# A fused MLP forward and backward: one load for each tile of x in two queues, w1's first part divided, and Gelu's table moved

## The chip, the cores and the metric

The kernel runs on one core of a Trainium2 chip. The metric is the device time of one execution in microseconds (us), the median of several runs; lower is better. The core has a matrix engine (TensorE, PE in the profile; PEld is its loading of weights), a vector engine (VectorE, DVE), an engine for activation functions (ScalarE, ACT), a general one (GpSimd, POOL) and a queue engine that only issues transfers (SyncE, SP). Transfers (DMA) are issued here by SP and by ScalarE, each in a queue of its own, in order.

## The reference

A two-layer MLP with the tanh form of Gelu, and the gradients of all its inputs, in bfloat16, with 2048 rows, width 448 and hidden width 1792:

```python
def _fwd_reference(x, w1, b1, w2, b2):
    h = jnp.einsum("bsd,df->bsf", x, w1) + b1
    h = _gelu(h)
    return jnp.einsum("bsf,fd->bsd", h, w2) + b2

def reference(x, w1, b1, w2, b2, grad_out):
    _out, _vjp = jax.vjp(_f, x, w1, b1, w2, b2)
    return (_out, *_vjp(grad_out))      # out, gx, gw1, gb1, gw2, gb2
```

## The kernel before

The hidden width is cut into 14 tiles of 128, taken two at a time (a pair, 7 of them), and the rows into 4 blocks of 512. That gives 28 pairs p = 0 to 27. For each pair there is a step `u` (x times w1 into PSUM), a bias copy `c` into a buffer, Gelu `g` on ScalarE, a step `p` or `o` (h times w2), a step `q` (the gradient times w2 transposed), the derivative of Gelu on ScalarE and VectorE (`s e r y t z m n G`), and `x` (the gradient of h times w1 transposed). The weight gradients follow at the end, with full 128-row matmuls (L798, L852).

The order on each engine is written out by hand in five strings: `PE_ORDER`, `ACT_ORDER`, `DVE_ORDER`, `SP_ORDER` and a few names for GpSimd. An engine runs its string from left to right and waits where an input is not there or a buffer is not free. Nothing is reordered. A step `u2.1` is pair 2, first of two runs (d = 1), `u2.2` its second (d = 2). The width of 448 is not a multiple of 128, so TensorE works with its array cut into two halves of 64 rows; two matmuls of a run stand side by side, and a run has 4 such pairs of matmuls for d = 1 and 3 for d = 2 while p is below 7.

This case is about the start. Pair 0 is not done as `u0` with 512 columns but as `h0` and `h1`, with 256 columns each (the first and the second 256 rows of x), so that it can begin before all of the first block is there. The names at the start:

- `xr01`: the load of tile 0 of x (128 rows, 112 KB) into `x_rows`; `xr12` is tile 1, `xr24` tiles 2 and 3 in one load. They are issued by the engine in whose string they stand.
- `X0` to `X3` in `PE_ORDER`: TensorE turns a tile of x with an identity matrix into two PSUM banks: `X_BANKS = ((0, 1), (2, 3), (6, 7), (0, 1))`. `X3` uses the banks of `X0`.
- `X0.0`, `X0.1` and so on in the strings of VectorE and ScalarE: the copy of one of the two banks into `xT` (L600). VectorE has X0.0 X1.0 X3.0 X3.1, ScalarE X0.1 X1.1 X2.0 X2.1.
- `W6`: six matmuls with ones, to have TensorE running; `F6` and `f4`: fills, six and four pairs of small matmuls with ones into PSUM columns that nothing reads.
- `L0` to `L4`: w1's five parts by columns (256, 256, 256, 256, 768), for pairs 0, 1, 2, 3 and 4 to 6. `Z0` to `Z2`: the rest of w1's rows, by `REST_COLS`; a step `u` of the first block needs the `L` and the `Z` of its pair.
- `K`, `J`, `I`: parts of w2, w2 transposed and w1 transposed. `b1` is loaded by SP, turned by TensorE in `B`, and copied by VectorE as `b1T`; the bias copies `c0A0` (ScalarE) and `c0B0` (VectorE) need it.
- `table`: an ACTIVATE of one column with Gelu, so that the table of the function is loaded early.
- `HOLD`: a load named in it waits until another one has landed. Here `L1` (`w11m`), issued by SP, waits for the first rows of x (`xrows0`), and SP issues nothing else meanwhile.

`Nx` and `Ng` (`rows_nat`, L732) load all of x and of grad_out again, for the weight gradients, in two halves each.

Of the kernel before, what the change touches and what calls it, by code (L numbers as in the profile page):

```python
# [88 lines left out]


PE_ORDER = """
W6 X0 X1 F6 X2 X3 h0.1 f4 h0.2 B h1.1 u1.1 h1.2 u1.2 u2.1 u3.1 u2.2 u3.2 p0.0 p0.1 p0.2 p0.3 p1.0 p1.1 u4.1 u5.1 u4.2 u5.2
p1.2 p1.3 p2.0 p2.1 p2.2 p2.3 u6.1 p3.0 u6.2 p3.1 p3.2 p3.3 p4.0 p4.1 u7.1 p4.2 u7.2 p4.3 p5.0 p5.1 p5.2 p5.3 u8.1
p6.0 u8.2 q0.1 p6.1 q0.2 u9.1 p6.2 u9.2 q1.1 p6.3 q1.2 u10.1 o1.0.0.6.1 u10.2 q2.1 o1.1.0.6.1 u11.1 q2.2 u11.2
o1.0.0.6.2 o1.1.0.6.2 q3.1 u12.1 q3.2 u12.2 o1.0.6.10.1 q4.1 o1.1.6.10.1 u13.1 q4.2 u13.2 o1.0.6.10.2 q5.1 o1.1.6.10.2
# [11 lines left out]
x3.1.6.10.1 x3.0.6.10.2 x3.1.6.10.2 x3.0.10.14.1 x3.1.10.14.1 x3.0.10.14.2 x3.1.10.14.2  # L107
"""
ACT_ORDER = """
xr12 L0 Z0 table X0.1 X1.1 X2.0 X2.1 c0A0 c0A1 s0 g0 s1 g1 c2B t0 s2 g2 g3 s3 c5B g4 t1 t2 c6B g5 g6 s4 s5 g7 c8A c8B g8 c9A c9B  # L110
g9 c10A c10B t3 t4 g10 s6 c11A c11B s7 g11 t5 c12A c12B g12 s8 t6 c13A c13B g13 s9 t7 s10 t8 c14A c14B t9 g14 s11 s12
c15A c15B t10 g15 c16A c16B s13 t11 g16 c17A c17B s14 t12 g17 c18A c18B s15 g18 vx0.2 c19A c19B t13 t14 g19 s16 c20A
c20B s17 g20 t15 s18 t16 s19 c21A c21B t17 g21 c22A c22B s20 t18 g22 c23A c23B g23 s21 t19 s22 t20 s23 c24A c24B t21
# [12 lines left out]
vx3.3  # L126
"""
SP_ORDER = """
xr01 xr24 b1 L1 Z1 L2 L3 K0 K1 L4 Z2 K2 K3 X1 R F b2 Y0 J0 J1 J2 Y1 I0 E J3 I1 So0.1 So0.0 X2 H0 H1 H2 H3 H4 H5 H6 H7 H8 H9
T0 T1 H10 T2 H11 T3 H12 T4 H13 T5 So1.0 So1.1 T6 T7 H14 T8 Y2 H15 T9 X3 H16 T10 H17 Sx0.0 Sx0.1 T11 H18 H19 T12 H20  # L130
T13 T14 T15 So2.0 Y3 H21 So2.1 T16 H22 H23 T17 T18 T19 H24 Sx1.0 T20 Sx1.1 H25 T21 H26 Nx H27 T22 T23 Sx2.0 Sx2.1 T24
T25 T26 So3.0 So3.1 Ng T27 Sx3.0 Sx3.1
# [28 lines left out]
def make_plan(tc, ctx, x, w1, b1, w2, b2, grad_out, out_0, out_1, out_2, out_3, out_4, out_5):  # L161
    nc = tc.nc
    P = 128
    _, S, D = x.shape
    F = w1.shape[1]
# [3 lines left out]
    MAIN = 3 * P  # L169
# [201 lines left out]
    def fill(n, bks, c0):  # L371
        def fn():
            run(n * [[(bks[i], (c0, P), one[64 * i:64 * i + 64, 0:P], one[64 * i:64 * i + 64, 0:P], True, True) for i in (0, 1)]], True)
        pe("fill", fn, [], [bank(("fill", len(pl.lists["PE"]), i), bks[i]) for i in (0, 1)], ("s128", n), (bks, 1))
# [143 lines left out]
        return {"SP": nc.sync, "ACT": nc.scalar, "POOL": nc.gpsimd}[eng]  # L518

    loads = {}  # L520
    HOLD = {"w11m": "xrows0"}

    def dma(eng, name, out, in_, reads, writes, nbytes):
        def fn():
            d = loads[name] = dq(eng).dma_start(out=out, in_=in_)
# [82 lines left out]
        v += [val((tag[0] + "e", b), (tag + "e", b % 2))] if b > 0 else []  # L608
        turn_rows(f"{tag}{b}.{hs[0]}", dst[b % 2][:, :, EDGE + c0 - e:EDGE + c0 + n], src, b * SB + c0 - e, n + e, v, tag if b == NB - 1 else None)

    def LW1(part, eng="SP"):
        c0, c1 = W1_COLS[part]
        v = [("w1", part)]
        dma(eng, f"w1{part}m", w1_sb[:, 0:3, c0:c1], w1[0:MAIN, c0:c1].rearrange("(k p) f -> p k f", p=P), [], v, (c1 - c0) * 768)

    def LW1Z(part, eng="SP"):

# [40 lines left out]
    def num(t):  # L658
        return [int(i) for i in t.split(".")]

    for t in PE_ORDER.split():
        k, a = t[0], t[1:]
        if k == "w":
            wake(int(a), P)
        elif k == "W":
            wake(int(a))
        elif k == "X":
            XT(int(a))
        elif k == "f":
            fill(int(a), (3, 2), 2 * P)  # L670
        elif k == "F":
            fill(int(a), (6, 7), 2 * P)
        elif k == "B":
            pe("b1u", lambda: nc.tensor.matmul(bk_(6)[:, 0:16], lhsT=b1n[0:64, :], rhs=ident[0:64, 0:16], start=True, stop=True,  # L674
                                               skip_group_check=True), ["b1n", "b1z", "ident"], [bank(("b1u",), 6)], ("s16", 1), (None, 0))
# [22 lines left out]
    for eng, order in (("ACT", ACT_ORDER), ("DVE", DVE_ORDER)):  # L698
        for t in order.split():
            k, a = t[0], t[1:]  # L700
            if k == "c":
                hf = None if a[-1] in "AB" else int(a[-1])
                a = a if hf is None else a[:-1]
                C(int(a[:-1]), "AB".index(a[-1]), eng, hf)
            elif k == "v":
                EV(a[0], *num(a[1:]), eng)
            elif k == "L":
                LW1(int(a), eng)
            elif k == "Z":
                LW1Z(int(a), eng)  # L710
            elif t[:2] == "xr":
                LXN(int(t[2]), int(t[3]), eng)
            elif t == "ident":
                pl.op(eng, "ident", identity, ["identz"], ["ident"], ("tiny", 1))
            elif k == "X":
                XC(*num(a), eng)
            elif k == "D":
                LED({"x": "xT", "g": "gT"}[a[0]])
            elif k == "K":
                LW2(int(a), eng)  # L720
            elif t in ("b1", "b2"):
                (LB1 if t == "b1" else LB2)(eng)
            elif t == "b1T":
                pl.op(eng, "b1T", b1_turn, [("b1u",)], ["b1T"], ("tiny", 4))
            elif t == "table":
                pl.op(eng, "table", lambda: nc.scalar.activation(out=tiny[:], in_=one[:, 0:1], func=ACT.Gelu_apprx_tanh), [], ["tiny"], ("table", 1))
# [66 lines left out]
    for ft in range(NF):  # L793
# [7 lines left out]
        eng = "ACT"  # L801
# [94 lines left out]
```

## Time and profile before

| | |
|---|---|
| median of 3 runs | 264.36 us (264.32 to 264.71) |
| profiled execution | 264.21 us |
| its span, first to last instruction | 262.4 us |
| TensorE busy | 259.0 us (99%) |
| VectorE busy | 199.3 us (76%) |
| ScalarE busy | 127.3 us (48%) |
| DMA | 46.61 MB, mean 178 GB/s |

The span is what the profiler saw between the first and the last instruction; the execution's own time has about 1.8 us around it. A row of a timeline gives the start in us from the span's start, the duration, the engine (a q behind it: its queue, issuing), the line of the kernel, the operation, what it writes and reads, its shape (64*128 64x512: a weight of 64 by 128 against 512 columns), how many instructions were merged, and in brackets the idle time before it and what ended it. A row of stretches gives, for each, its length and each engine's busy time. In `qb` lie PSUM banks 6 and 7; `bank` is any of the other six; `TR` holds x's first rows at the start; `w1f` holds w1, `gh_nat` at first the rest of its rows (`Z`).

### The profile page before, as it was taken

The numbers are of one execution on the slowest core, as the hardware profiler recorded it, in microseconds if no ns is written. First come the engines' busy times: TensorE is split into PE (matmuls) and PEld (weight loads), VectorE is DVE, ScalarE is ACT, GpSimd is POOL, SyncE is SP. The second block draws the span as 40 slices with busy tenths as digits, with TensorE's granted clock in tenths as the row PEclk, the third lists the DMA queues.
The fourth block names the chain that finished last, engine by engine and source line by source line (L and its number), as shares of the span: only waits on it lengthen the run. The fifth ranks groups of instructions, "written<-read, shape, count | busy, mean of one in ns | idle before, by whom it ended". The sixth has DMA issues, their size and how long they took to land.

```text
span 262.4 us, 5411 instructions
## 1 busy us (share of the span) xinstructions
PE 259.0 (99%) x2217; PEld 149.0 (57%) x2217; DVE 199.3 (76%) x286; ACT 127.3 (48%) x165; POOL 14.2 (5%) x11
## 2 busy tenths in 40 slices
PE   8999999999999999999999999999999999999995
PEld 4444455555555666666666677765555555555554
DVE  5898398999999989999997995249999999310000
ACT  4899569846898956875896310011121111000001
POOL 1000000000000000000000000000000392400000
PEclk9999999999999999999999999999999999999999
DMA  6999999999999892992387825984799989877221
GB/s 187 306 261 147 204 134 152 244 352 215 256 208 220 233 232 45 163 235 43 102 207 250 222 42 62 243 238 95 157 238 125 180 194 179 200 179 178 72 70 35
DMA packets 120633, 46.61 MB, mean 178 GB/s; under 512 B 96686, under 2 KB 120479, under 8 KB 120608
## 3 DMA queue, kind: packets, MB, share of 16 engines
q1 hardware_dynamic: 119920, 45.82, 79.1%
q10 hardware_dynamic: 688, 0.44, 0.5%
q8 instruction: 17, 0.28, 0.4%
q14 instruction: 8, 0.07, 0.1%
HBM read 8.20 MB, written 14.28 MB: 86 GB/s over the span
## 4 chain that ended last, share of the span: by engine, by line
PE 99%; ACT 0%; issue 0%
PE bank L242 48%; PE qb L242 18%; PE bank L798 16%; PE bank L852 16%; PE qb L368 1%; ACT w_sb L857 0%; PE qb L674 0%
## 5 line engine op out<-in xcount | busy, mean ns | idle before, releaser
L242 PEld LDWEIGHTS <-HG 64*128 64x128 bf16 x896 | 55.6, 94 | 32.2 <-POOLq L236 1.9
L242 PE MATMUL qb<-gT,w2Tf 64*128 64x512 bf16 x392 | 52.9, 376 | 0.0
L242 PE MATMUL bank<-w_sb,HG 64*128 64x448 bf16 x448 | 48.4, 349 | 0.0
L242 PE MATMUL bank<-xT,w1f 64*128 64x512 bf16 (+1 forms) x360 | 47.6, 370 | 0.0
L242 PE MATMUL bank<-w1T_sb,HG 64*128 64x448 bf16 x448 | 47.2, 349 | 0.0
L482 DVE SCALAR_TENSOR_TENSOR HG<-TR,qb 128x1024 bf16<-128x1024 bf16 x28 | 34.1, 1218 | 12.6 <-PE qb L242 12.5
L852 PE MATMUL bank<-w2Tf,HG 128*128 128x448 bf16 (+2 forms) x240 | 42.6, 340 | 0.0
L798 PE MATMUL bank<-w1f,gh_nat 128*128 128x448 bf16 x224 | 42.5, 352 | 0.0
L852 PEld LDWEIGHTS <-HG 128*128 128x128 bf16 x240 | 22.9, 98 | 19.8
L798 PEld LDWEIGHTS <-gh_nat 128*128 128x128 bf16 x224 | 21.8, 98 | 20.6 <-issue 0.4
L242 PEld LDWEIGHTS <-w2Tf 64*128 64x128 bf16 x392 | 24.1, 94 | 16.6 <-POOLq L236 0.3
L467 ACT ACTIVATE TR<-TR 128x1024 bf16<-128x1024 bf16 x28 | 29.1, 1052 | 6.6 <-DVE TR L457 6.6
L242 PEld LDWEIGHTS <-w1f 64*128 64x128 bf16 x382 | 21.7, 94 | 17.7 <-DMA w1f<-in_w_dram 0.7
L821 DVE TENSOR_TENSOR w1T_sb<-w1T_sb,gh_nat 128x1792 f32<-128x1792 f32 x14 | 28.4, 2026 | 0.5
L803 ACT ACTIVATE TR<-bank 128x448 bf16<-128x448 f32 x14 | 7.6, 543 | 34.9 <-PE bank L798 34.9
L858 DVE CAST w_sb<-bank 128x448 bf16<-128x448 f32 x6 | 3.7, 623 | 25.9 <-PE bank L852 25.9
L857 ACT CAST w_sb<-bank 128x448 bf16<-128x448 f32 (+2 forms) x9 | 4.4, 490 | 37.7 <-PE bank L852 37.7
L827 POOL PARTITION_ALL_REDUCE w1T_sb<-w1T_sb x1 | 10.6, 10568 | 206.2 <-DVE w1T_sb L825 206.2
L442 ACT ACTIVATE TR<-gh_nat 128x1024 bf16<-128x1024 bf16 x15 | 15.7, 1052 | 11.5 <-DVE TR L477 11.5
L472 DVE TENSOR_SCALAR TR<-TR 128x2048 bf16<-128x2048 bf16 x28 | 19.2, 688 | 1.9 <-ACT TR L467 1.9
L462 DVE TENSOR_TENSOR TR<-TR,HG 128x1024 bf16<-128x1024 bf16 x28 | 19.2, 684 | 0.0
L477 DVE TENSOR_TENSOR TR<-TR 128x1024 bf16<-128x1024 bf16 x28 | 19.0, 686 | 0.1
(55 smaller groups left out, 188.9 us busy)
## 6 DMA issues: line engine op xcount, KB each, us to landing
hT_dram<-HG SPq DMA_DIRECT2D x28, 256.0 KB, 3.0
out_dram<-st SPq DMA_DIRECT2D x16, 224.0 KB, 2.8
w1f<-in_x_dram SPq DMA_DIRECT2D x2, 896.0 KB, 5.9
w2Tf<-in_grad_out_dram SPq DMA_DIRECT2D x2, 896.0 KB, 6.4
out_dram<-w_sb SPq DMA_DIRECT2D x2, 448.0 KB, 3.0
out_dram<-xT SPq DMA_DIRECT2D x2, 384.0 KB, 3.2
w_sb<-in_w_dram SPq DMA_DIRECT2D x1, 672.0 KB
w1f<-in_w_dram SPq DMA_DIRECT2D x3, 192.0 KB, 3.7
```

The source lines that it names most:

```text
L242: m = nc.tensor.matmul(bk_(b)[:, at:at + n], lhsT=l, rhs=r, start=st, stop=sp, skip_group_check=True)
L442: pl.op("ACT", f"s{p}", lambda: nc.scalar.activation(out=TR[p % NTR][:, 1], in_=ubuf(p), func=ACT.Square, scale=sc), [("ub", p)], [v], ("a ...
L462: pl.op("DVE", f"R{p}", lambda: nc.vector.tensor_tensor(out=t[:, 1], in0=t[:, 1], in1=hblk(p), op=ALU.mult), [("r", p), ("h", p)], [val((" ...
L467: pl.op("ACT", f"t{p}", lambda: nc.scalar.activation(out=t[:, 0], in_=t[:, 0], func=ACT.Tanh), [("y", p)], [val(("t", p), ("TR0", p % NTR) ...
L472: pl.op("DVE", f"m{p}", lambda: nc.vector.tensor_scalar(out=t[:], in0=t[:], scalar1=1.0, scalar2=None, op0=ALU.subtract), [("t", p), ("r2" ...
L477: pl.op("DVE", f"n{p}", lambda: nc.vector.tensor_tensor(out=t[:, 0], in0=t[:, 0], in1=t[:, 1], op=ALU.mult), [("m0", p), ("m1", p)], [val( ...
L482: pl.op("DVE", f"G{p}", lambda: nc.vector.scalar_tensor_tensor(out=ghblk(p), in0=t[:, 0], scalar=2.0, in1=qb[:, :, :], op0=ALU.subtract, o ...
L798: nc.tensor.matmul(bk_(bk)[:, 0:D], lhsT=gh_nat[:, st // 4, ft, st % 4, :], rhs=x_nat[:, st, :], start=(st == 0), stop=(st == NS - 1))
L803: fn = (lambda dst=dst, src=src: nc.scalar.mul(out=dst, in_=src, mul=-0.5)) if eng == "ACT" else \
L821: nc.vector.tensor_tensor(out=hs3, in0=a, in1=gh_nat[:, st // 4, :, st % 4, :], op=ALU.add)
L827: pl.op("POOL", "gb1", lambda: nc.gpsimd.partition_all_reduce(gb1_w, hsum, channels=P, reduce_op=bass_isa.ReduceOp.add), ["hsc"], ["gb1"], ...
L852: nc.tensor.matmul(bk_(bk)[:, 0:d1 - d0], lhsT=h_nat[ft][:, st, :], rhs=g_nat[:, st, d0:d1], start=(st == 0), stop=(st == NS - 1))
```

## The change

- x's four tiles are loaded by one load each: tiles 0 and 2 by SP, 1 and 3 by ScalarE, ahead of all else in both queues.
- w1's first part `L0` is divided: `L0a` (two of its three blocks of rows, 128 KB) third in SP's queue, `L0b` (the third, 64 KB) third in ScalarE's.
- `Z0` covers 256 columns (pair 0) instead of 512, `Z1` 768 instead of 512; both are now issued by ScalarE. `b1` goes behind `L1`.
- Nothing is held any more: `HOLD` is empty.
- `table` moves behind ScalarE's four copies of x.
- On TensorE, `F6` becomes `F3`, `f4` goes ahead of `h0.1` (and into banks 5 and 4, which h0 uses, instead of 3 and 2), and `h1.1` goes ahead of `h0.2`.
- `Nx` and `Ng` are one load each instead of two.

```diff
 PE_ORDER = """
-W6 X0 X1 F6 X2 X3 h0.1 f4 h0.2 B h1.1 u1.1 h1.2 u1.2 u2.1 ...
+W6 X0 X1 F3 X2 X3 f4 h0.1 h1.1 h0.2 B u1.1 h1.2 u1.2 u2.1 ...
 ACT_ORDER = """
-xr12 L0 Z0 table X0.1 X1.1 X2.0 X2.1 c0A0 c0A1 s0 g0 ...
+xr12 xr34 L0b Z0 Z1 X0.1 X1.1 X2.0 X2.1 table c0A0 c0A1 s0 g0 ...
 SP_ORDER = """
-xr01 xr24 b1 L1 Z1 L2 L3 K0 K1 L4 Z2 K2 K3 X1 ...
+xr01 xr23 L0a L1 b1 L2 L3 K0 K1 L4 Z2 K2 K3 X1 ...
...
-    REST = (0, 0, 1, 1, 2, 2, 2)
-    REST_COLS = ((0, 512), (512, 1024), (1024, F))
+    REST = (0, 1, 1, 1, 2, 2, 2)
+    REST_COLS = ((0, 256), (256, 1024), (1024, F))
...
-    HOLD = {"w11m": "xrows0"}
+    HOLD = {}
...
-    def LW1(part, eng="SP"):
+    def LW1(part, eng="SP", k0=0, k1=3):
         c0, c1 = W1_COLS[part]
         v = [("w1", part)]
-        dma(eng, f"w1{part}m", w1_sb[:, 0:3, c0:c1], w1[0:MAIN, c0:c1].rearrange("(k p) f -> p k f", p=P), [], v, (c1 - c0) * 768)
+        dma(eng, f"w1{part}m{k0}", w1_sb[:, k0:k1, c0:c1], w1[k0 * P:k1 * P, c0:c1].rearrange("(k p) f -> p k f", p=P), [], v, (c1 - c0) * 256 * (k1 - k0))
...
         elif k == "f":
-            fill(int(a), (3, 2), 2 * P)
+            fill(int(a), (5, 4), 2 * P)
...
+            elif t == "L0b":
+                LW1(0, eng, 2, 3)
...
-        for s0, s1 in ((0, 8), (8, 16)):
+        for s0, s1 in ((0, 16),):
...
+        elif t == "L0a":
+            LW1(0, "SP", 0, 2)
```

More of the change, by code (lines that the diff above doesn't have):

```diff
@@ L91 @@
 PE_ORDER = """
-W6 X0 X1 F6 X2 X3 h0.1 f4 h0.2 B h1.1 u1.1 h1.2 u1.2 u2.1 u3.1 u2.2 u3.2 p0.0 p0.1 p0.2 p0.3 p1.0 p1.1 u4.1 u5.1 u4.2 u5.2
+W6 X0 X1 F3 X2 X3 f4 h0.1 h1.1 h0.2 B u1.1 h1.2 u1.2 u2.1 u3.1 u2.2 u3.2 p0.0 p0.1 p0.2 p0.3 p1.0 p1.1 u4.1 u5.1 u4.2 u5.2
 p1.2 p1.3 p2.0 p2.1 p2.2 p2.3 u6.1 p3.0 u6.2 p3.1 p3.2 p3.3 p4.0 p4.1 u7.1 p4.2 u7.2 p4.3 p5.0 p5.1 p5.2 p5.3 u8.1
@@ L109 @@
 ACT_ORDER = """
-xr12 L0 Z0 table X0.1 X1.1 X2.0 X2.1 c0A0 c0A1 s0 g0 s1 g1 c2B t0 s2 g2 g3 s3 c5B g4 t1 t2 c6B g5 g6 s4 s5 g7 c8A c8B g8 c9A c9B
+xr12 xr34 L0b Z0 Z1 X0.1 X1.1 X2.0 X2.1 table c0A0 c0A1 s0 g0 s1 g1 c2B t0 s2 g2 g3 s3 c5B g4 t1 t2 c6B g5 g6 s4 s5 g7 c8A c8B g8 c9A c9B
 g9 c10A c10B t3 t4 g10 s6 c11A c11B s7 g11 t5 c12A c12B g12 s8 t6 c13A c13B g13 s9 t7 s10 t8 c14A c14B t9 g14 s11 s12
@@ L128 @@
 SP_ORDER = """
-xr01 xr24 b1 L1 Z1 L2 L3 K0 K1 L4 Z2 K2 K3 X1 R F b2 Y0 J0 J1 J2 Y1 I0 E J3 I1 So0.1 So0.0 X2 H0 H1 H2 H3 H4 H5 H6 H7 H8 H9
+xr01 xr23 L0a L1 b1 L2 L3 K0 K1 L4 Z2 K2 K3 X1 R F b2 Y0 J0 J1 J2 Y1 I0 E J3 I1 So0.1 So0.0 X2 H0 H1 H2 H3 H4 H5 H6 H7 H8 H9
 T0 T1 H10 T2 H11 T3 H12 T4 H13 T5 So1.0 So1.1 T6 T7 H14 T8 Y2 H15 T9 X3 H16 T10 H17 Sx0.0 Sx0.1 T11 H18 H19 T12 H20
```

## The prediction, made before the changed kernel was run

> **What bounds the kernel now.** I read the page first: the span, the busy shares and the chain that ended last.
>
> ```profile
> span 262.4 us, 5411 instructions
> ...
> PE 259.0 (99%) x2217; PEld 149.0 (57%) x2217; DVE 199.3 (76%) x286; ACT 127.3 (48%) x165; POOL 14.2 (5%) x11
> ...
> PE 99%; ACT 0%; issue 0%
> ```
>
> TensorE is busy for 99% and is the whole chain, so nothing is to be had from another engine as such; only a hole in TensorE's row, or work that TensorE does for nothing, can be won or lost. Second view: the stretches, to see where holes can be.
>
> ```profile
> core 0: us, PE busy (x) PEld busy (x) DVE busy (x) ACT busy (x) POOL busy (x), PEclk, DMA share, GB/s
> 9.21:174.83 165.62, 165.61 (x1644) 100.06 (x1644) 141.49 (x231) 110.12 (x133) 0.00 (x0) 1.00 0.86 192
> 174.83:259.80 84.97, 84.97 (x466) 44.73 (x464) 52.60 (x38) 12.29 (x23) 13.44 (x2) 1.00 0.71 151
> ...
> 2.40:4.30 1.90, 1.90 (x31) 0.89 (x29) 0.92 (x4) 1.73 (x4) 0.00 (x0) 1.00 1.10 356
> ...
> 6.30:7.50 1.20, 1.20 (x18) 0.62 (x16) 0.47 (x1) 0.46 (x1) 0.00 (x0) 1.00 0.98 229
> ```
>
> From 9.21 us to 259.80 TensorE is busy for 250.58 of 250.59 us. That is a rigid block of matmuls: the end comes 253.2 us after its first one, the start of u3.1. So the question is one number: **when does u3.1 start?** Third view: the timeline of TensorE's matmuls up to there.
>
> ```profile
> 0.76 2.72 PE L368 MATMUL qb<-const-bfloat16-1.0 128*128 128x512 bf16 x6 [0.76 <-PEq L880]
> 3.41 0.56 PE L242 MATMUL bank<-st,TR 64*128 64x64 bf16 x16
> 3.81 0.51 PE L242 MATMUL qb<-const-bfloat16-1.0 64*128 64x128 bf16 x12
> 4.35 0.29 PE L242 MATMUL qb<-st,TR 64*128 64x64 bf16 x8
> 4.48 0.28 PE L242 MATMUL bank<-st,TR 64*128 64x64 bf16 x8
> 4.78 0.50 PE L242 MATMUL bank<-xT,w1f 64*128 64x256 bf16 x6
> 5.11 0.27 PE L242 MATMUL bank<-xT,gh_nat 64*128 64x256 bf16 x2
> 5.22 0.39 PE L242 MATMUL bank<-const-bfloat16-1.0 64*128 64x128 bf16 x8
> ...
> 5.84 0.17 PE L674 MATMUL qb<-st,b1n 64*128 64x16 bf16 x1
> ...
> 6.33 0.82 PE L242 MATMUL bank<-xT,w1f 64*128 64x512 bf16 x6
> ...
> 8.18 0.81 PE L242 MATMUL qb<-xT,w1f 64*128 64x512 bf16 x6
> 8.83 0.38 PE L242 MATMUL qb<-xT,gh_nat 64*128 64x512 bf16 x2
> 9.22 0.82 PE L242 MATMUL bank<-xT,w1f 64*128 64x512 bf16 x6
> ```
>
> In order: the wake-up W6 (0.76), the transposes X0 X1, the fill F6 (3.81), X2, X3, then h0.1 (4.78), f4 (5.22), h0.2, B (5.84, it turns b1), h1.1, u1.1 (6.33), h1.2, u1.2, u2.1 (8.18), u3.1 (9.22). Two matmuls run side by side on the two halves of the array, so I count pairs. Three pairs of 256 columns take 5.11 - 4.78 = 0.33 us, 0.11 each; three of 512 take 8.83 - 8.18 = 0.65, 0.216 each. A d = 1 run has four pairs, a d = 2 run three. u1.1 to the end of u2.1 is therefore 0.86 + 0.33 + 0.65 + 0.86 = 2.7, and u3.1 could have started at 9.05; it started at 9.22.
>
> What ended TensorE's waits, by the weight loads; when SP issued L1, held until the first rows were there; and what w1's first loads took (KB, us from issue to landing):
>
> ```profile
> 4.35 0.29 PEld L242 LDWEIGHTS <-TR 64*128 64x128 bf16 x16 [0.21 <-DMA TR<-in_x_dram]
> ...
> 9.21 0.33 PEld L242 LDWEIGHTS <-w1f 64*128 64x128 bf16 x6 [0.50 <-DMA w1f<-in_w_dram]
> ```
>
> ```profile
> 3.30 0.40 SPq L525 DMA_DIRECT2D w1f<-in_w_dram  x1
> ```
>
> ```profile
> w1f<-in_w_dram ACTq DMA_DIRECT2D x1, 192.0 KB, 3.6
> gh_nat<-in_w_dram ACTq DMA_DIRECT2D x1, 128.0 KB, 3.4
> ```
>
> x's third and fourth tile (one load) end the wait at 4.35, and w1's part L3 that at 9.21, 0.17 us after TensorE was free. ScalarE's and VectorE's rows of the same microseconds, and between them the group of ScalarE's copies (busy us, mean ns of one):
>
> ```profile
> 0.72 0.41 ACTq L525 DMA_DIRECT2D TR<-in_x_dram  x1
> 1.15 0.46 ACTq L525 DMA_DIRECT2D w1f<-in_w_dram  x1
> 1.65 0.53 ACTq L525 DMA_DIRECT2D gh_nat<-in_w_dram  x1
> 2.21 1.28 ACT L726 ACT_TABLE_LOAD   x1 [2.21 <-issue]
> 3.50 0.20 ACT L726 ACTIVATE tiny<-const-bfloat16-1.0 128x1 bf16<-128x1 bf16 x1
> 3.87 0.65 ACT L600 CAST xT<-bank 128x256 bf16<-128x256 f32 x2 [0.16 <-PE bank L242]
> ...
> 6.29 0.47 ACT L417 ACTIVATE ub<-bank,b1T 128x256 bf16<-128x256 f32 x1 [0.96 <-DVE b1T L695]
> ...
> 8.35 1.06 ACT L442 ACTIVATE TR<-ub 128x1024 bf16<-128x1024 bf16 x1
> ```
>
> ```profile
> L600 ACT CAST xT<-bank 128x256 bf16<-128x256 f32 x2 | 0.6, 375 | 0.2 <-PE bank L242 0.2
> ```
>
> ```profile
> 3.84 0.76 DVE L600 CAST xT<-bank 128x256 bf16<-128x256 f32 x2 [0.95 <-PE bank L242]
> 4.80 0.76 DVE L600 CAST xT<-bank 128x256 bf16<-128x256 f32 x2 [0.20 <-PE bank L242]
> ```
>
> The reader is to see two things. The copies of X0 and X1 are over at 3.84 + 0.76 = 4.60, so of the start at 4.78 only 0.18 us is owed to w1's first part (issued 1.15, landed 3.6 later, 4.75): a quicker load alone can't bring more. And ScalarE is ready for its first copy only at 3.70, 0.17 before it is needed.
>
> **The change, part by part.**
>
> *ScalarE's queue.* Three issues take from 0.72 to 2.21, 0.5 each. Five take to 0.72 + 5 x 0.5 = 3.2. They stand ahead of everything else on ScalarE.
>
> *The table.* The load of 1.28 us had no wait of its own and stood directly ahead of the first instruction of ScalarE's own. Behind the change the first one is a copy. Where the load goes can't be read from this trace; between its ends (it stays at `table`: nothing ahead of the copies; it stays ahead of the first instruction: 1.28) I take the second, because that is what the row shows: the load came ahead of ScalarE's first instruction, and a copy is one. Then, whether or not Gelu needs another one later, X0.1 starts at 3.2 + 1.28 + 0.01 = 4.49 instead of 3.87. Two copies take 0.65 and one 0.375, so they start 0.27 apart: X0.1 ends at 4.87, X1.1 at 5.14, X2.0 at 5.41, X2.1 at 5.68.
>
> The Trainium skill, page "ScalarE: Activation LUTs", section "Table sets: the hidden batching unit", says that copy and other cheap functions are in every table set and that a load is put before every activation that needs one. By that a copy, too, wants some set to be active, and any would do; with it the sum is the forecast's, without it the faster rival's below. The trace has no copy ahead of a load and can't tell.
>
> *TensorE's transposes.* X0 and X1 stay at 3.41 (tile 0 is still the first load of SP's queue). F3 instead of F6 gives back half of 0.35 us that lay inside the wait to 4.35 anyway: nothing. X2's tile now comes in a load of its own, no later than the 4.35 of the old pair. But X3 writes the banks of X0 (0 and 1) and waits for X0.1: 4.87 + 0.05 = 4.92 instead of 4.48. Its four pairs end at 5.04; f4 (0.23 for four pairs of 128 columns) ends at 5.27; X1.1 is ready at 5.2, so h0.1 starts at 5.27 instead of 4.78. f4 is covered: what follows is later still.
>
> *The new order h0.1 h1.1 h0.2.* h1.1 needs all four tiles. VectorE began X3's copies 0.32 after X3's start (4.48 to 4.80) and took 0.76: 4.92 + 0.32 + 0.76 = 6.00. h0.1 has ended at 5.71, so TensorE waits 0.34 us and h1.1 runs from 6.05 to 6.49, h0.2 to 6.82. Queued behind the wait are B, u1.1 and everything else. u1.1 starts at 6.82 instead of 6.33.
>
> *The loads.* Before, 640 KB (x and w1's first part) had landed by 4.75, and 768 KB by 1.65 + 3.4 = 5.05. L0a, L0b and the smaller Z0 complete 704 KB: about 4.9, under 5.27. L1 and Z1, 393 thousand bytes more, take 1.1 us at the 356 GB/s of two queues or 1.7 at the 229 of one: 6.0 to 6.6, under 6.82. b1, behind L1 on SP, is there by then; B needs it at 6.8. L2 and L3 add 0.9 us each at 229: 8.4 at the latest for L3, under 9.5. So without HOLD no load of w1 is waited for, and the 0.17 us ahead of u3.1 goes. L1 was issued at 3.30 and is now SP's fourth issue, at about 2.2, so SP is some 1.1 us ahead from then on; nothing on TensorE waits for SP after 9.21, so that is worth nothing.
>
> *u3.1.* 6.82 + 2.70 = 9.52 against 9.22: **+0.3 us.**
>
> *Does the block stay rigid?* c0A0 waits for b1T, 0.45 after B (5.84 to 6.29 before): 7.27. If Gelu's table is a second load, it stands behind X2.1: 5.68 + 1.28 + 0.20 = 7.17, hidden by 0.1 us. Everything that follows u1.1 is 0.49 later, the row of ScalarE work that starts at 8.35 with it. It is needed here:
>
> ```profile
> 11.20 1.04 ACT L437 ACTIVATE HG<-ub 128x1024 bf16<-128x1024 bf16 x1
> ```
>
> ```profile
> 11.38 2.44 PE L242 MATMUL bank<-w_sb,HG 64*128 64x448 bf16 x24
> 13.65 0.81 PE L242 MATMUL qb<-xT,w1f 64*128 64x512 bf16 x6
> ```
>
> g1 ends at 12.24 and p1.0, nine pairs into the stretch (0.19 each), starts at 12.9: 0.66 in hand. After, g1 at 12.73 and p1.0 at 13.2: 0.5 in hand. Nothing stalls.
>
> *The rest.* REST's new columns move bytes between Z0 and Z1 and are counted above. One load of x_nat and of g_nat instead of two saves an SP issue each, long before TensorE needs them: at 174.83 it goes on with no hole to speak of. Nothing.
>
> Sum: the profiled execution took 264.21 us (262.4 and 1.8 around), so 264.5; the median of the runs shown lies 0.15 higher, so **264.7**.
>
> **The rivals.**
>
> *Faster: the copies need no table.* Then the load stays at `table`, X0.1 runs at 3.87 and X3 follows X2 at 4.3 instead of 4.48. h0.1 starts at about 4.7 to 4.9 by w1's landing, h1.1 at 5.45 (X3's copies, 4.3 + 0.32 + 0.76), u1.1 at 6.22 and u3.1 at 8.92: 0.3 us less, 264.1. If h1.1 never waited it would be 4.66 + 3.9 = 8.56: 0.65 less, 263.7. For it: only ACTIVATE is seen behind a load. Against: one load ahead of everything is all that the trace has.
>
> *Slower: Gelu's load lands on the path.* It has 0.1 us of cover, then 0.5 at p1.0. If the second switch takes twice its row, 2.57, c0A0 starts at 8.45 and s0 at 9.4, g1 ends at 13.3 and p1.0 waits 0.1; each further tenth costs a tenth. Time 264.8 to 265.2, decided from a switch of about 2.5 us on. Against: in the row ACTIVATE follows the load by 0.01 us. The Trainium skill, same page, section "What ACT_TABLE_LOAD costs", gives 1283 ns, with which the trace's 1.28 us agrees, and a drain of 1380 ns beside it, which the trace's 0.01 does not show; by the page g1 would be another 0.1 later.
>
> *Slower: the clock.* It was granted in full (PEclk 1.00) in all the stretches quoted, with holes of 0.2 us. After, they are 0.8 (4.1 to 4.92) and 0.34. The six wake-up matmuls took 0.45 each against 0.216 at 4.78 and after: half the clock, for the first 3.4 us. If the holes lose the clock for as long, half of 3.4 is lost: 266.4.
>
> **How the numbers follow.** Forecast 0.61 (264.4 to 265.0), faster rival 0.18, Gelu's load 0.17, clock 0.04. The range 264.0 to 265.2 leaves out the clock, and the far ends of the others. 0.2% of 264.36 is 0.53 us, about what a measurement of this kernel can tell from no change: below 263.83 lies a third of the faster rival, 0.06; above 264.89 a fifth of the forecast, half of Gelu's load and the clock, 0.12 + 0.08 + 0.04 = 0.24; 0.70 between.
>
> **What would show it.** In the changed kernel's timeline: an ACT_TABLE_LOAD at about 3.2, ahead of the first CAST, and X0.1 at 4.5; X3 at 4.9; h1.1 at 6.05 after a wait for VectorE's copy; u3.1 at 9.5 with no DMA wait before it; TensorE full from there. A CAST at 3.87 with no load ahead makes it wrong on the fast side; ScalarE's first bias copy later than 7.3, or a PEclk under 1.00 after 4 us, on the slow side.

## The result and the profile after

The changed kernel takes **265.16 us** (median of 16 runs, 264.99 to 266.89), the kernel before 264.30 beside it (16 runs, 263.97 to 264.79): 0.86 us less. The ratio of the means is 1.005, with a 95% interval of 1.0033 to 1.0067 (the ratios below, too, weigh the highest runs in). It is slower by half a per cent in the mean and by 0.3% in the median; the forecast was 264.7 and no change that can be told. The range, 264.0 to 265.2, just holds the median. The 16 times fall in two groups: ten from 264.99 to 265.21, which is 0.8 us above before, and six from 266.29 to 266.89, another 1.6 us up. Both have to be explained. The profiled execution (265.11 us) belongs to the first.

The page of the changed kernel: span, busy time by engine, and the chain that ended last by engine.

```profile
span 263.3 us, 5399 instructions
...
PE 258.7 (98%) x2211; PEld 148.8 (57%) x2211; DVE 199.2 (76%) x286; ACT 128.5 (49%) x166; POOL 14.2 (5%) x11
...
PE 97%; DMA 1%; ACT 1%; issue 0%; DVE 0%; ACTq 0%
```

The chain that was TensorE for 99% now has 1% of DMA and 1% of ScalarE in it. A second load of a table adds its 1.28 us to ScalarE's busy time (127.3 to 128.5); that alone says nothing of the end. The stretches from the new start of u3.1 show whether the loss lies ahead of it or behind:

```profile
10.06:175.68 165.62, 165.62 (x1646) 99.67 (x1642) 141.54 (x232) 110.31 (x133) 0.00 (x0) 1.00 0.83 189
175.68:260.65 84.97, 84.97 (x466) 44.73 (x464) 52.60 (x38) 12.30 (x23) 13.44 (x2) 1.00 0.71 151
```

TensorE is busy for 250.59 of 250.59 us, as before (250.58 of 250.59). So the block stayed rigid, and all of the loss is u3.1's start: 10.06 instead of 9.22. TensorE's timeline up to there, and ScalarE's:

```profile
3.41 0.49 PE L242 MATMUL bank<-st,TR 64*128 64x64 bf16 x16
...
4.30 0.19 PE L242 MATMUL bank<-st,TR 64*128 64x64 bf16 x1
5.47 0.27 PE L242 MATMUL bank<-st,TR 64*128 64x64 bf16 x7 [0.98 <-ACT xT L600]
5.57 0.40 PE L242 MATMUL bank<-const-bfloat16-1.0 64*128 64x128 bf16 x8
5.85 0.50 PE L242 MATMUL bank<-xT,w1f 64*128 64x256 bf16 x6
...
6.58 0.50 PE L242 MATMUL bank<-xT,w1f 64*128 64x256 bf16 x6
...
7.36 0.83 PE L242 MATMUL bank<-xT,w1f 64*128 64x512 bf16 x6
...
10.06 0.83 PE L242 MATMUL bank<-xT,w1f 64*128 64x512 bf16 x6
```

```profile
2.13 1.59 ACTq L525 DMA_DIRECT2D gh_nat<-in_w_dram  x2
3.75 1.28 ACT L600 ACT_TABLE_LOAD   x1 [3.75 <-DMA TR<-in_x_dram]
5.05 0.65 ACT L600 CAST xT<-bank 128x256 bf16<-128x256 f32 x2
...
6.26 1.28 ACT L728 ACT_TABLE_LOAD   x1
7.56 0.21 ACT L728 ACTIVATE tiny<-const-bfloat16-1.0 128x1 bf16<-128x1 bf16 x1
7.85 0.47 ACT L417 ACTIVATE ub<-bank,b1T 128x256 bf16<-128x256 f32 x1
```

There are two table loads. The first (3.75) stands ahead of the first copy, at the copy's own line L600; the second (6.26) ahead of Gelu. The copy X0.1 runs at 5.05, and X3's second matmul, which writes the bank that X0.1 empties, at 5.47. h0.1, h1.1, u1.1 and u3.1 follow at 5.85, 6.58, 7.36 and 10.06. The chain that ended last (start, us, what) says how they hang together:

```profile
0.72 2.65 DMA TR<-in_x_dram
...
3.39 0.33 ACTq L525
...
3.75 1.28 ACT L600
...
5.05 0.38 ACT xT L600
...
6.11 0.42 DVE xT L600
```

It runs from the landing of a tile of x through an issue of ScalarE, the table's load, X0.1 and VectorE's copies of X3 to h1.1. The first row of ScalarE says what is new: two issues that take 0.5 us each took 1.59. The fifth issue, Z1's, stood still for 0.8 us, from 2.6 to 3.39. In the program as it was built, in the order of the instructions and with what each waits for (no times in it), ScalarE's queue reads

```
1 L525 DMA TR_80<-in_x_dram 128x448 x2
2 L525 DMA w1f<-in_w_dram 128x256
3 L525 DMA gh_nat<-in_w_dram 128x256
4 L525 DMA gh_nat<-in_w_dram 128x768 [waits DMAHW0_49]
5 L600 ACT_TABLE_LOAD
```

and SP's, from its fifth issue on, names DMAHW1, 2, 3 and so on to 7. A semaphore is a counter by which a landing is told. In this program eight of them serve the loads of both queues in turn; Z1 is the ninth load, so its issue waits until the load of the first turn (x's tile 1, the first on ScalarE) has landed, at 3.37 by the chain. Z1's issue, 0.33 us long, ran until 3.72 (2.13 + 1.59). The table's load, which needs nothing from any of this, is queued behind it.

w1's first part is late too, though here it is covered. Its loads (KB, us from issue to landing):

```profile
w1f<-in_w_dram SPq DMA_DIRECT2D x1, 128.0 KB, 4.2
w1f<-in_w_dram ACTq DMA_DIRECT2D x1, 64.0 KB, 3.9
gh_nat<-in_w_dram ACTq DMA_DIRECT2D x1, 64.0 KB, 3.9
```

Issued at 1.63, 1.64 and 2.13, they landed at about 5.8, 5.5 and 6.0; before, the whole of w1's first part (192 KB in one load) landed at 4.75 and a `Z0` of twice the size at 5.05. h0.1 began at 5.85, less than 0.1 us behind the later of the first two; its last pair alone needs the third. h0.1 isn't what holds h1.1, though: h1.1 waits for VectorE's copies of X3 until 6.58, about 0.3 us after h0.1 is done, so w1 could have come 0.3 us later at no cost. The bytes moved in the same stretch (last column, GB/s), before and after:

```profile
3.50:4.50 1.00, 0.97 (x38) 0.79 (x40) 0.66 (x2) 0.84 (x3) 0.00 (x0) 1.00 1.05 320
```

```profile
3.50:4.50 1.00, 0.88 (x31) 0.69 (x32) 0.67 (x2) 0.75 (x1) 0.00 (x0) 1.00 0.55 157
```

Half the rate, at the time when w1's first part is wanted; in the microsecond after it the change has 316 and the kernel before 214. The kernel before has such a stretch too, shorter and later:

```profile
4.30:5.00 0.70, 0.65 (x22) 0.50 (x22) 0.49 (x2) 0.53 (x3) 0.00 (x0) 1.00 0.64 150
```

So there were two candidates for the 0.84 us: the late copies (theory A: the table's load behind the held issue), and the late part of w1 (theory B). They end close together, and the chain shows only the one that ended last, the copies. For the six runs above 266 a third (theory D): TensorE does so little from 4.3 to 5.5 us that the full clock is granted later.

### The profile page after: what moved, and what is told of

It is laid out like the page before. It is cut to its first block, busy times and chain, and to the rows that moved or that the text cites. A ratio compares the mean times of both kernels' runs of the same rounds, so it can differ in the third digit from the quotient of the medians.

```text
span 263.3 us, 5399 instructions
## 1 busy us (share of the span) xinstructions
PE 258.7 (98%) x2211; PEld 148.8 (57%) x2211; DVE 199.2 (76%) x286; ACT 128.5 (49%) x166; POOL 14.2 (5%) x11
## 4 chain that ended last, share of the span: by engine, by line
PE 97%; DMA 1%; ACT 1%; issue 0%; DVE 0%; ACTq 0%
PE bank L242 47%; PE qb L242 17%; PE bank L802 16%; PE bank L856 16%; DMA TR<-in_x_dram 1%; ACT L600 0%; DVE xT L600 0%; ACT xT L600 0%; ACTq L525 0%; ACT w_sb L861 0%; PE qb L674 0%
```

## The experiments

Each edit is to the changed kernel, for b1 and b2 to the kernel before. In the expectations A, B and D are the theories above. F is that w1's first part is late by its place behind x, H that its division makes it late, G that L1, no longer held, takes its bytes, and J that both queues read w1 in pieces of 512 bytes (256 columns) at the same time. Each was timed beside runs of the kernel before on the same chip, whose medians were (264.30 beside the change itself) 264.36 (a1, b2, a2, a3), 264.47 (c1, c2, a4, b1) and 264.48 (c4, a5, c3, d1).

**The copies on time, by moving Z1.** Four issues on ScalarE instead of five.

```diff
-xr12 xr34 L0b Z0 Z1 X0.1 X1.1 X2.0 X2.1 table c0A0 ...
+xr12 xr34 L0b Z0 X0.1 X1.1 X2.0 X2.1 table c0A0 ...
-xr01 xr23 L0a L1 b1 L2 ...
+xr01 xr23 L0a L1 Z1 b1 L2 ...
```

> The changed kernel, with Z1 issued by SP (behind L1) instead of by ScalarE, so that ScalarE has four issues and none of them waits. Theory A (ScalarE's copies are late: a table load of 1.28 us behind the issues, itself held by Z1's issue, which waited until 3.37 us for x's tile 1 to land): the load starts at about 2.6 instead of 3.75, X0.1 at 3.9 instead of 5.05; if that is all, u3.1 starts about 1.1 us earlier and the time is 264.0 to 264.2. Rival B (w1's first part, divided, lands late by itself: 5.5 to 5.8 in the changed kernel): X0.1 is early, yet h0.1 still starts at about 5.8, h1.1 follows it without a wait, u3.1 starts at about 9.75 and the time is 264.8 to 264.9.

Measured: 265.06 (7 runs: four from 264.80 to 265.06, three from 266.46 to 266.82), ratio 1.0053 (1.0029 to 1.0076). ScalarE's row and that of TensorE's weights:

```profile
2.64 1.28 ACT L600 ACT_TABLE_LOAD   x1 [2.64 <-issue]
3.94 0.65 ACT L600 CAST xT<-bank 128x256 bf16<-128x256 f32 x2
```

```profile
5.60 0.34 PEld L242 LDWEIGHTS <-w1f 64*128 64x128 bf16 x6 [0.68 <-DMA w1f<-in_w_dram]
```

The load came at 2.64, X0.1 at 3.94, 1.1 us earlier, nearly where it was before (3.87). Yet h0.1 started only 0.25 us earlier, at 5.60, and now it waits for w1. The lower four runs (median 264.87) are 0.2 us under the lower ten of the change (265.09), or 0.3 us counted from the kernel before beside each. A is not enough; B stands right behind it. How far behind differs between executions: with the change's own order of loads, w1's first part landed at 5.6 to 6.3 in the five traces that have it (the change, a2, a3, a4, d1), so a difference of a few tenths between two single traces is not certain.

**The copies on time, by the order of the turns.** L1 is held again, as before, until x's first tile has landed. That alters the program's order of loads, and with it which of them has to wait for a turn.

```diff
-    HOLD = {}
+    HOLD = {"w11m0": "xrows0"}
```

> The changed kernel with L1 held until x's first tile has landed, as before the change; nothing else. Eight loads share eight semaphores, and with L1 later Z1 is the eighth load instead of the ninth, so ScalarE's issue of Z1 should no longer wait. Theory A: Z1 is issued at about 2.6 instead of 3.39, the first table load runs from 3.15 instead of 3.75, X0.1 at 4.5 instead of 5.05, as the prediction had it. Then theory G (w1's divided first part lands late because L1 shares the transfers) gives a first part at about 4.9, h0.1 at 5.3, u3.1 at 9.5 and 264.5; rival J (it lands late because both queues read w1 in pieces of 512 bytes at the same time) gives 5.3 to 5.6 for it, u3.1 at 9.7 and 264.6 to 264.8.

Measured: 264.89 (12 runs: eight from 264.66 to 264.96, four from 266.53 to 266.83), ratio 1.0035 (1.0015 to 1.0055). The profiled execution is one of the upper four (266.79), which makes it useful twice. ScalarE first:

```profile
2.12 0.96 ACTq L525 DMA_DIRECT2D gh_nat<-in_w_dram  x2
3.11 1.28 ACT L600 ACT_TABLE_LOAD   x1 [3.11 <-issue]
4.41 0.65 ACT L600 CAST xT<-bank 128x256 bf16<-128x256 f32 x2
```

Z1 no longer waits: two issues in 0.96 us, the load at 3.11 and X0.1 at 4.41. These are the prediction's 3.2 and 4.49. So the turn of the semaphores is worth 0.6 us of ScalarE's time (3.75 against 3.11), and nothing else was wrong with that step. TensorE:

```profile
4.83 0.37 PE L242 MATMUL bank<-st,TR 64*128 64x64 bf16 x7 [0.23 <-ACT xT L600]
...
5.86 0.82 PE L242 MATMUL bank<-xT,w1f 64*128 64x256 bf16 x6 [0.23 <-DMA w1f<-in_w_dram]
6.47 0.42 PE L242 MATMUL bank<-xT,gh_nat 64*128 64x256 bf16 x2
...
8.18 1.51 PE L242 MATMUL bank<-xT,w1f 64*128 64x512 bf16 x6
...
10.93 0.82 PE L242 MATMUL qb<-xT,w1f 64*128 64x512 bf16 x6
11.80 0.82 PE L242 MATMUL bank<-xT,w1f 64*128 64x512 bf16 x6
```

h0.1 starts at 5.86, the same as in the changed kernel, with another wait in front: w1. L1 was held and w1's part still came no sooner, later than G (4.9) or J (5.3 to 5.6) had it, at 207 GB/s in the stretch from 3.5 to 4.5 us. That does not decide against G: with L1 held, Z1, as large (192 KB), was issued at 2.6 instead of 3.39 and shares the transfers in its place. What is gained comes after it, where h1.1 no longer waits for VectorE's copies of X3: at full clock u1.1 would be 11 pairs of 0.11 behind h0.1, at 7.07 instead of 7.36, 0.29 us earlier. The lower eight runs have a median of 264.80, 0.3 us under the lower ten of the change; counted from the kernel before beside each, 0.3 us are left of 0.8. The rest of this fence belongs to the clock, below.

**The table.** Ahead of the copies in the changed kernel, behind them in the kernel before.

```diff
-xr12 xr34 L0b Z0 Z1 X0.1 X1.1 X2.0 X2.1 table c0A0 ...
+xr12 xr34 L0b Z0 Z1 table X0.1 X1.1 X2.0 X2.1 c0A0 ...
```

> The changed kernel, with the table's ACTIVATE put back ahead of ScalarE's copies of x (behind its five issues). Theory A (a load stands ahead of the first copy either way): one table load, at 3.75, and X0.1 0.2 us later than in the changed kernel, 5.25: the time is 0.2 us longer, 265.3 to 265.4. Rival C (the move of the table, by its second load, is what costs): the time goes back to 264.3 to 264.6.

Measured: 265.82 (6 runs: three from 265.24 to 265.28, three from 266.35 to 266.49), ratio 1.0056 (1.0039 to 1.0073). ScalarE:

```profile
3.88 1.28 ACT L728 ACT_TABLE_LOAD   x1 [3.88 <-DMA TR<-in_x_dram]
...
5.28 0.63 ACT L600 CAST xT<-bank 128x256 bf16<-128x256 f32 x2
```

One load, still behind the held issue; X0.1 0.23 later than in the changed kernel (0.13 because the held issue ended later in this execution, 0.10 for the small ACTIVATE that now stands ahead of it) and the lower runs about 0.2 us later.

```diff
-xr12 L0 Z0 table X0.1 X1.1 X2.0 X2.1 c0A0 ...
+xr12 L0 Z0 X0.1 X1.1 X2.0 X2.1 table c0A0 ...
```

> The kernel before, with nothing but the table's ACTIVATE moved behind ScalarE's four copies of x. Theory A: two table loads, the first at 2.21 as before, so X0.1 at 3.87 as before; the second at 5.35, over at 6.85 with its ACTIVATE, so c0A0 at 6.85 instead of 6.29, which c0A1 at 7.73 hides; u3.1 and the time as before, 264.2 to 264.5. Rival C (the second load costs): 0.3 us or more longer.

Measured: 264.61 (11 runs, ten from 264.08 to 264.92 and one at 266.41), ratio 1.0008 (0.9994 to 1.0023). ScalarE:

```profile
2.21 1.28 ACT L600 ACT_TABLE_LOAD   x1 [2.21 <-issue]
3.87 0.65 ACT L600 CAST xT<-bank 128x256 bf16<-128x256 f32 x2 [0.38 <-PE bank L242]
...
5.58 1.28 ACT L726 ACT_TABLE_LOAD   x1
```

Two loads, and X0.1 at 3.87 as before. The profiled execution (264.78) starts u3.1 at 9.78, because it had half the clock until 6.45 us, not because of the table: nothing on TensorE waits for ScalarE's second load. What costs time is not where Gelu's table stands but when ScalarE is done with its issues.

**Where w1's first part stands.** Undivided, in ScalarE's queue, second (ahead of x's tile 3) or third (behind it); L1 and Z1 on SP in both.

```diff
-xr12 xr34 L0b Z0 Z1 X0.1 ...          (SP: xr01 xr23 L0a L1 b1 L2 ...)
+xr12 L0 xr34 Z0 X0.1 ...              (SP: xr01 xr23 L1 Z1 b1 L2 ...)
```

> The changed kernel with w1's first part whole again and second in ScalarE's queue, as before the change (xr12 L0 xr34 Z0), and Z1 on SP, so that ScalarE has four issues. Theory F (the divided first part lands at 5.3 to 5.8 because it stands third in both queues, behind all of x, with L1 at its heels): L0 lands at 4.7 to 4.9 as before, tile 3 at about 4.4; with X0.1 at 3.95 h0.1 starts at about 4.9, h1.1 at 5.7, u3.1 at 9.1 to 9.2, and the time is 264.1 to 264.5. Rival G (without HOLD, SP's L1 shares the transfers and any first part lands late): L0 at 5.3 or later, u3.1 at 9.5 or later, 264.7 and above.

Measured: 265.68 (7 runs: four from 265.19 to 265.68, three from 266.77 to 267.69), ratio 1.0071 (1.0044 to 1.0098). The weights' row:

```profile
5.51 0.17 PEld L242 LDWEIGHTS <-TR 64*128 64x128 bf16 x8 [1.43 <-DMA TR<-in_x_dram]
```

w1's first part was there in time (landed at 4.4), and nothing waited for it: second it lands at 4.4, third (c2, next) at 6.8, so its place in the queue decides when it comes. But x's tile 3, behind it, came only at about 5.5, beside L1, and holds X3 until 5.51. Neither theory had that.

```diff
-xr12 xr34 L0b Z0 Z1 X0.1 ...          (SP: xr01 xr23 L0a L1 b1 L2 ...)
+xr12 xr34 L0 Z0 X0.1 ...              (SP: xr01 xr23 L1 Z1 b1 L2 ...)
```

> The same, but with w1's first part, whole, third in ScalarE's queue (xr12 xr34 L0 Z0); Z1 on SP. Theory F (the place in the queue): it lands at 5.3 to 5.8 like the divided one, h0.1 starts then, 264.7 to 264.9. Rival H (the division over two queues): whole, it lands at 4.9 although it is third, 264.2 to 264.4.

Measured: 265.95 (4 runs, 265.63 to 266.30), ratio 1.0059 (1.0042 to 1.0075).

```profile
6.84 0.22 PEld L242 LDWEIGHTS <-w1f 64*128 64x128 bf16 x6 [1.67 <-DMA w1f<-in_w_dram]
```

Undivided and third, it is later still, and later than either theory had it (L1 and Z1, 384 KB, were under way on SP beside it). So it isn't the division that makes w1's first part late (H). It is its place behind two tiles of x, with the other queue's loads of w1 beside it.

**The hold.** Nothing held, in the kernel before:

```diff
-    HOLD = {"w11m": "xrows0"}
+    HOLD = {}
```

> The kernel before, with nothing changed but that L1 is not held. Theory F: L0 lands at 4.7 to 4.9, L1 at about 5.5 instead of 6.3 and L3 at about 8.5 instead of 9.17, so the 0.17 us ahead of u3.1 and the 0.05 ahead of u1.1 go: 264.0 to 264.3. Rival G (L1 shares the transfers with the first loads): L0 or x's tiles 2 and 3 land 0.3 us or more later, h0.1 starts at 5.1 or later, and the time is 264.4 to 264.7.

Measured: 264.31 (11 runs, 264.11 to 264.88), ratio 0.9999 (0.999 to 1.0008).

```profile
4.87 0.50 PE L242 MATMUL bank<-xT,w1f 64*128 64x256 bf16 x6
...
6.52 0.83 PE L242 MATMUL bank<-xT,w1f 64*128 64x512 bf16 x6
```

L1's bytes put h0.1 0.09 and u1.1 0.19 us later, and the wait of 0.17 ahead of u3.1 is gone: nothing is left over. By itself the hold is worth nothing, in that order of loads.

L1 held with Z1 moved to SP, the two repairs of ScalarE's row together:

```diff
-    HOLD = {}
+    HOLD = {"w11m0": "xrows0"}          (and a1's two strings)
```

> The changed kernel with Z1 on SP and L1 held until x's first tile has landed: ScalarE has four issues and X0.1 runs at 3.95, and only L0a, L0b and Z0 are under way behind x. Theory G (L1's sharing): the first part lands at 4.9, u3.1 starts at about 9.1, 264.1 to 264.4. Rival J (two queues in w1 at once): it lands at 5.3 or later, as without the hold (5.3 to 5.6), u3.1 at 9.5 or later, 264.6 to 264.9.

Measured: 265.24 (10 runs, 264.96 to 265.40), ratio 1.0027 (1.0018 to 1.0036).

```profile
5.28 0.50 PE L242 MATMUL bank<-xT,w1f 64*128 64x256 bf16 x6 [0.43 <-DMA w1f<-in_w_dram]
...
7.53 0.17 PE L674 MATMUL qb<-st,b1n 64*128 64x16 bf16 x1 [0.88 <-DMA b1n<-in_b_dram]
```

w1's first part came 0.3 us earlier than without the hold (a1, one trace each), so L1's bytes cost something (G), but it still did not come by 4.9, with neither L1 nor Z1 ahead of it or beside it until 3.3; that much is left for J or another cause. TensorE then waited for b1, which I had left behind L1 and Z1 in SP's queue. The time therefore says nothing of the hold; the row at 5.28 does.

L0 second, L1 held, b1 ahead of it:

```diff
-xr12 xr34 L0b Z0 Z1 X0.1 ...          (SP: xr01 xr23 L0a L1 b1 L2 ...)
+xr12 L0 xr34 Z0 X0.1 ...              (SP: xr01 xr23 b1 L1 Z1 L2 ...)
-    HOLD = {}
+    HOLD = {"w11m0": "xrows0"}
```

> The changed kernel's one load for each tile, its order on TensorE, its three fills and its table behind the copies, but w1's first part whole and second in ScalarE's queue, L1 held until x's first tile has landed, b1 ahead of it and Z1 on SP. If the late table load and w1's late first part are the whole cost (theories A with G or J), L0 lands at about 4.5, tile 3 at 4.4, h0.1 starts at about 4.9, u3.1 at 9.1 to 9.3, and the time is that of the kernel before, 264.1 to 264.5. Rival: something else in the change costs (the order h0.1 h1.1 h0.2, the single loads), and it stays at 264.7 or above.

Measured: 264.75 (11 runs, 264.40 to 265.19), ratio 1.0012 (1.0003 to 1.002).

```profile
4.88 0.23 PEld L242 LDWEIGHTS <-TR 64*128 64x128 bf16 x8 [0.49 <-DMA TR<-in_x_dram]
```

With w1's first part back in second place, L1 held and no fifth issue on ScalarE, all but 0.3 us of the loss is gone, and no run is above 265.2. But 264.75 lies on the rival's side of its 264.7, so the rival (something else in the change costs) is not ruled out: the rest of the change (the table, the new order on TensorE, the fills, x in four loads, `Nx` and `Ng`) may cost up to 0.2% together. Tile 3, now behind w1's first part, holds X3 until 4.88 instead of 4.48, and in the new order h0.2, B and u1.1 stand behind h1.1, which needs X3's copies; an estimate from these rows (4.88 + 0.32 + 0.76 + 0.05 for h1.1, 0.77 more for u1.1) gives u1.1 at 6.78 against 6.33 and, without the 0.17 ahead of u3.1, a loss of 0.28 us. The profiled execution (265.03) also had half the clock until 6.63. No run puts the old order back.

**The clock.** A fill in the hole ahead of X3, long and short, and then a shorter wake-up. First twenty pairs.

```diff
-W6 X0 X1 F3 X2 X3 f4 h0.1 ...
+W6 X0 X1 F3 X2 f20 X3 f4 h0.1 ...
```

> The changed kernel, with 20 pairs of fill (1.16 us) between X2 and X3, inside the hole of 1.3 us in which TensorE waits for X0.1. Theory D (6 of the 16 runs of the changed kernel lie at 266.3 to 266.9, because TensorE did too little in its first microseconds and was granted its full clock one period of 3.4 us later): the runs at 266.3 and above are gone, and the others stay at 265.0 to 265.2; before the full clock comes the fill would be slower than it is at full clock, so a run or two at 265.5 may be left. Rival E (the upper group has another cause, in the transfers say): about a third of the runs stay at 266.3 to 266.9.

Measured: 265.69 (5 runs, 265.28 to 265.90), ratio 1.0049 (1.0037 to 1.0061).

```profile
4.36 2.06 PE L242 MATMUL bank<-const-bfloat16-1.0 64*128 64x128 bf16 x40
```

Twenty pairs take 2.06 us, against 20 x 0.058 = 1.16 at full clock (four pairs in 0.23): most of them ran at half, and the fill itself is in the way. No run is above 265.90. Nine pairs instead:

```diff
-W6 X0 X1 F3 X2 X3 f4 h0.1 ...
+W6 X0 X1 F3 X2 f9 X3 f4 h0.1 ...
```

> The changed kernel with 9 pairs of fill between X2 and X3: 0.5 us at the full clock and 0.96 at half, so that they fit into the hole of 1.3 us at either. Theory D (TensorE, idle for most of 4.1 to 5.5 us, is in some executions found too idle and gets its full clock one period of 3.4 us later): the runs at 266.3 and above are gone, the others stay at 265.0 to 265.2. Rival E (another cause): about a third of the runs stay at 266.3 to 266.9.

Measured: **265.17, all 9 runs from 265.07 to 265.25**, ratio 1.0026 (1.0016 to 1.0036). The upper group is gone, and nothing else is: this is the lower group of the change. c1, timed beside it, has three of seven runs in its upper group. Then the other way, two wake-up matmuls instead of six:

```diff
-W6 X0 X1 F3 X2 X3 f4 h0.1 ...
+W2 X0 X1 F3 X2 X3 f4 h0.1 ...
```

> The changed kernel with two wake-up matmuls instead of six, so that TensorE is idle from 1.6 to 3.4 us. Theory D (the full clock is granted at the end of a period of 3.4 us in which TensorE did enough, wherever that period falls): fewer executions get it by 4 to 6 us, most get it at 6.5 us or later, and the times go to 266 to 267 with few or none at 265.1; the trace shows pairs of 256 columns at 0.21 us instead of 0.11. Rival E (the upper group of 266.3 to 266.9 has nothing to do with the clock): the times stay as they are, two thirds at 265.1.

Measured: 266.61 (4 runs, 266.19 to 267.37), ratio 1.0082 (1.0066 to 1.0098): all of them up. In the trace:

```profile
6.12 0.87 PE L242 MATMUL bank<-xT,w1f 64*128 64x256 bf16 x6
6.76 0.45 PE L242 MATMUL bank<-xT,gh_nat 64*128 64x256 bf16 x2
```

Three pairs of 256 columns take 0.64 us, 0.213 each, against 0.11 in the kernel before: half clock. The same is seen in the fence of the held kernel above: three pairs of 256 columns in 6.47 - 5.86 = 0.61, and six matmuls of 512 from 8.18 on in 1.51 us, but in 0.82 from 10.93 on, as before. That execution had half the clock until about 10 us, and u3.1 came at 11.80; the profiled execution of the changed kernel had the full clock from 3.64 us on (0.11 a pair at 5.85). No upper execution of the changed kernel itself was traced; by a5's and d1's traces the upper group is the same program with the full clock granted later, at 9.2 to 10 us instead of before 7.

A fill in the hole takes the group away, a shorter wake-up makes it the rule. The length of the hole alone does not decide: a1, whose trace has a wait of only 0.41 us ahead of h0.1, has three of seven runs in it, and c3, with waits of 0.43 and 0.88, none of ten. `F3` in place of `F6` takes work from TensorE as well, and no run puts `F6` back. How much TensorE must do to get the clock is open.

## Why the prediction was wrong

The path was right: table, X0.1, X3, VectorE's copies, h1.1, u1.1. Its first term was mis-sized, ScalarE's five issues, by 0.5 us, and that takes the time past the 264.89 above which the prediction counted a run as slower. A second term, the landing of w1's first part, was off by 0.9 us and stood right behind it. A third, the clock, was given too small a chance.

- **"Five take to 0.72 + 5 x 0.5 = 3.2": wrong.** The fifth issue waited 0.8 us for a turn, a wait that the prediction did not have, and ended at 3.72; the load began at 3.75. Everything behind it on the path shows the same shift:

| step | predicted | after | difference |
|---|---|---|---|
| table's load | 3.2 | 3.75 | 0.55 |
| X0.1 | 4.49 | 5.05 | 0.56 |
| X3 (bank of X0.1) | 4.92 | 5.47 | 0.55 |
| h0.1 | 5.27 | 5.85 | 0.58 |
| h1.1 | 6.05 | 6.58 | 0.53 |
| u1.1 | 6.82 | 7.36 | 0.54 |
| u3.1 | 9.52 | 10.06 | 0.54 |

264.5 for the profiled execution and 0.55 more make 265.05; it took 265.11. The trace of before hides it: its ninth and later loads stood in SP's queue behind the held L1 and were issued from 4.27 on, when the first ones had landed. Where the changed kernel held L1 (a5), the same five issues ended at 3.1, as predicted.
- **"About 4.9" for w1's first part: wrong, by 0.9 to 1.1 us.** I took it from the bytes that had landed by 4.75 and by 5.05 before, as if bytes land at the same pace in whatever order. In the changed order the stretch from 3.5 to 4.5 us has 157 GB/s, and 122 to 228 in the experiments of that kind, against 320 before. On the path of the changed kernel it cost nothing more, because the copies were late by as much; it is why putting the copies right (a1, a5) brings back only 0.2 to 0.5 us of 0.8.
- **The table: right, with some luck.** I had to choose between two ends that the trace could not tell apart. A copy does take a table's load ahead of it, and Gelu takes a second one. The faster rival, which needed copies without a table, fell with the row at 3.75. The Trainium skill, page "ScalarE: Activation LUTs", section "What ACT_TABLE_LOAD costs", gives 1283 ns for the load, as both rows show (1.28), and a drain of 1380 ns beside it; after the first load the copy starts 0.01 to 0.02 us behind its end, so no drain is seen here.
- **Gelu's load hidden by 0.1 us: right.** The ACTIVATE behind it ended at 7.77; c0A0 started at 7.85, with VectorE's b1T. The slower rival of the second switch did not come, and g1 and p1.0 had no stall: the block is rigid.
- **The wait at h1.1, 0.34 predicted: right.** h1.1 came 0.73 behind h0.1, 0.78 was predicted, and VectorE's copy released it.
- **No load of w1 waited for at u3.1: right,** and so was the 0.17 that goes (b1 shows it too, given back at once).
- **The clock: the time about right, the mechanism wrong, far too small a chance.** 266.4 was named, with 0.04; six of 16 runs are there, at 266.3 to 266.9. I had asked whether a hole loses a clock already granted. In a5's and d1's traces it is granted later in the first place: matmuls take twice the time up to about 10 and 9 us, and the full time from there to the end. That 266.4 came near is luck in part, since I had priced another loss. The sign that I named, a PEclk under 1.00 after 4 us, could not have shown it: in a5 the column reads 1.00 from 3.5 to 8.5 us, where a pair of 256 columns takes 0.21, and it reads 1.00 in the stretch 2.40:4.30 of the kernel before, which begins with the wake-up at half clock. The Trainium skill, page "TensorE: Matmul & The Clock Gate", section "What's actually happening", has the clock at half until one busy window of 3413 ns is over, and the windows running freely, so that the moment differs from run to run. By it an execution that gets the clock one window later loses half a window, 1.7 us (an estimate from the page's figure); the groups are 1.6 apart, which agrees. The section's spread of plus or minus 500 ns does not: 1.6 us at half speed are more than 3 us of delay between runs of one kernel, and over the profiled executions of all the kernels here the moment lay anywhere from 3.5 us to 10.

So the step from 264.3 to the measured level is: 0.3 as forecast, 0.55 by the held fifth issue (with w1's first part close behind it), and in six runs of 16 another 1.6 us, put down to a later clock.

## What to carry to other kernels

An issue of a load is an instruction with a wait like any other: see in the built program which semaphore it counts on and waits for. Here eight serve both queues, so from the ninth load on an issue waits for the landing of the load eight before it, and everything behind it on that engine waits too. When two inputs of one step are moved together, work out both arrivals and not only the later one; a repair of one alone gains only the distance to the other. In the first ten microseconds, take work away from TensorE only with an eye on the clock: here a group of times 1.6 us up was there with the hole, gone with a fill in it, and had all runs when the wake-up was cut short.

## What the runs showed of the hardware

- **An issue that waits stops its engine.** The ninth load of the two queues together waited for the landing of the first, because this program has eight semaphores for them: 0.8 us on ScalarE (two issues took 1.59 with the wait, 0.96 when the turn was free). The Trainium skill, page "DMA: Bandwidth & Descriptors", section "Anatomy of one DMA — SWDGE (gpsimd) path", says that such a wait is on the issuing engine's side, not in the DMA engines; the row agrees, since it is ScalarE that stands.
- **The rate falls for about a microsecond where x ends and w1 begins.** 122 to 228 GB/s from 3.5 to 4.5 us where both queues turned to w1 together with their third loads (the changed kernel, a1 to a5, c2, c3, d1), 308 to 338 where one was still in x while the other was in w1 (before, b1, b2, c1); c4, with L1 held, lies between, at 249. With the same order of loads single executions differ, from 122 to 209 (the change, a2, a3, a4, d1). Two queues in w1 are not needed for it: the kernel before has the same fall a little later, 150 GB/s from 4.30 to 5.00, when SP's L1 begins and ScalarE's loads are ending. Why is open: the start of w1's loads, the pieces of 512 bytes, the same rows of one tensor, or the number of loads could each do it, and none was tried by itself.
- **A copy on ScalarE has a table's load ahead of it.** Gelu's table does not come with it, so a copy ahead of the first Gelu makes two loads of one (the change, 3.75 and 6.26; b2, 2.21 and 5.58); with `table` ahead of the copies there is one (a2, 3.88).
- **The moment of the full clock differs from execution to execution.** By the traces' record of the granted clock it came at 3.64 us in the profiled execution of the change, 3.80 before, 6.45 in b2, 6.63 in c4, 9.19 in d1 and 10.03 in a5. b2, which differs from before by the table alone, had one run of 11 at 266.41. Nine pairs of small matmuls in the hole made the upper group 0 of 9, two wake-up matmuls instead of six 4 of 4.

No version here beats the kernel before: the best are b1 at 0.9999 and c4 at 1.0012 of its time.
